# A fused retention and ELU feed-forward kernel: load costs, zero matmuls and opening order of its built-in planner

## The chip, the cores and the metric

The kernel runs on one core of one Trainium2 chip. The metric is the device time of one execution in microseconds (us), the median of several runs. Times inside an execution come from one profiled execution and count from its first instruction.

## What is computed

The reference, cut to what matters (alpha is 1):

```python
scores = (1 / sqrt(64)) * q @ k.T                 # q, k, v: batch 8, heads 8, seq 576, dim 64
Dmat   = where(rel >= 0, gamma[h] ** rel, 0.0)    # gamma[h] = 1 - 2 ** (-5 - h), rel = row - column
attn   = (scores * Dmat) @ v
x      = attn.transpose(0, 2, 1, 3).reshape(4608, 512)
h      = x @ w_in                                 # 512 x 2048
g      = where(h > 0, h, exp(min(h, 0)) - 1)
out    = g @ w_out                                # 2048 x 512, float32
```

It is a retention layer (linear attention with a decay for each head) and a feed-forward layer (FFN) behind it. Inputs and output are float32; the kernel's matmuls run in bf16.

## The kernel before

**Tiling.** The sequence of a batch is cut into two stretches of 256 positions and a tail of 64. An item is one stretch of one batch with all 8 heads; the tails of four batches form an item of their own. The four items of the first two batches are split into two units of four heads each, numbered 0 to 7; units 0 to 3 make the opening. Retention is computed in chunks of 64 positions: scores within a chunk, and a running state (the sum of k times v) that carries what lies before it. The decay is put into q and k by tables of exponentials.

**Steps of a unit n.** Loads ldq, ldk, ldv (256 KB each, queue SP, `load`, line 424, and `load_part`, line 387). Four scaled copies to bf16, cq0n, cq1n, ck0n, ck1n (line 550, POOL or DVE), and a copy of v, cvn (line 560). Two transpose steps Tn_0 and Tn_1 on TensorE, four transposes each (line 582), whose results cpn_0 and cpn_1 take from PSUM (line 588); units 5 to 7 are turned by transposing DMAs instead (trn, line 571). Then scores (scn), state (stn), masks on DVE (line 916), and the step ivn, which adds what the state and the scores with v give. For later units and items one step A does scores and state of the next and iv of the last. Two copies xc0, xc1 (line 952) put a unit's result into xt, the left operand of the FFN.

**FFN.** An FFN block has 256 rows of x (the last two 512). Step F1_b_p makes 256 columns of h for block b (8 matmuls); ACT takes the exponential (ex, line 1069), ACT or DVE a relu or the like (md), DVE combines them to g (line 1091). Step F2_b_t_f adds four matmuls of g with w_out to an output tile; a copy and a store follow. F1 of block 0 needs the xt copies of units 0 and 1; F1 of block 1 those of units 2 and 3.

**Weights.** w_in comes in five DMAs, wi0 (columns for F1_b_0), wi1 (F1_b_1), wi2 (F1_b_2 and 3), wi3 (F1_b_4 and 5), wi4 (6 and 7); w_out in four, wo0 to wo3. POOL issues all nine; they cast float32 to bf16 on the way (lines 477 to 498). Two one-element copies on POOL (line 400) wait for wo0 and wo2 and hold back the loads of units 4 and 6.

**The planner.** Nothing of the order is written out by hand. Every step is an `Op` with a cost for each engine that may do it, what it needs, and a rank. `Plan.run` (line 67) plays a list schedule with these costs at build time: on each engine that is free, the ready step of lowest rank starts (`pick`, line 100). It models the DMA queues too: a load enters 1.25 us after its issue, moves for its cost (`LD`, line 210, for a 256 KB load), and is told 0.55 us later. The result is only an order for each engine, and a choice of engine; on the chip each engine works through its list in that order and waits on semaphores for what a step needs.

`AT` (line 228) gives a due time to a named step: the plan doesn't start it sooner. `RANKS` shifts ranks. Neither waits for anything on the chip; they shape the order alone.

**Zero matmuls.** Where the plan has a gap on TensorE ahead of a step in its first 50 us, the emitting loop (lines 1210 to 1227) puts matmuls or transposes of a tile of zeros there, as fillers:

```python
gap = op.start - last if op.start < 50 and last else 0.0
...
if op.name.startswith("T"):
    for n in range(int(gap * 0.8 / 0.06)):
        pin(nc.tensor.transpose(spot[:, n % 4], zero[:, :P], ident))
elif spot is not None:
    for _ in range(int(gap * 0.8 / 0.06)):
        mm(spot[:, :P], zero[:, :P], zero[:, :P], start=True, stop=True)
```

Seven matmuls of 128x512 zeros ("warm") stand at the very start, and iv steps hold four of 64x64 as a fence. Both are apart from the fillers. All matmuls go through a helper and have line 277 in the profile; the filling transposes have line 1224.

Of the kernel before, what the change touches and what calls it, by code (L numbers as in the profile page):

```python
# [205 lines left out]
ISSUE = 0.65  # L206
JOINT = True
BD_ACT = 0.6
TWO, STEP = 2, 4
WI, WI1, LD = 1.3, 1.65, 0.84  # L210
MOST, MOSTU = 4, 3
ASKED = ("ldk0",)
BD_POOL = 0.46
# [11 lines left out]
UAPART = (5, 7)  # L225
HOLD = {"ldq4": "wo0", "ldq6": "wo2"}
VLATE = (0, 1)
AT = {"wi0": 6.0, "wi1": 10.2, "wi2": 9.4, "wi3": 11.6, "wi4": 15.0, "wo0": 17.4, "wo1": 17.4, "wo2": 19.3, "wo3": 33, "so_0_1_0_0": 74, "so_1_0_0_0": 74, "so_1_1_0_0": 74, "so_2_0_0_0": 76, "so_2_1_0_0": 81.47, "F2_3_1_0_0": 78.57, "st2": 14.97, "g_2_6": 63.17, "us7_1": 60.01, "F2_0_1_12_0": 46.64, "md_3_3": 66.87, "md_1_7": 35.82, "us5_0": 44.11, "ex_2_4": 55.85, "ex_2_2": 53.77, "xc1_u4": 43.93, "xc0_4": 82.16, "g_1_3": 27.7, "xc1_u3": 22.43, "F2_3_0_8_0": 78.02, "md_0_7": 36.11, "F1_6_6": 119.86, "tr0_5": 66.58, "md_2_2": 56.94, "ex_6_5": 119.61, "cq00": 5.78, "md_0_1": 21.97, "cp2_0": 11.19, "mask1_7": 117.16, "md_0_5": 25.96, "cp3_0": 15.79, "F2_4_0_8_0": 93.26, "cv7": 47.1, "sc1": 10.9}
RANKS = {"us1_0": -2, "F1_0_1": 4, "mask0_7": 2, "g_2_1": -2, "md_3_3": 8, "A7": -4, "cv1_5": -4, "cv1_6": 4, "mask1_u6": 8, "so_5_0_0_0": -8, "md_0_2": -8, "ex_2_7": 2, "xc0_u7": -8, "F1_2_6": -8, "A4": 2, "F2_3_0_4_0": -8}
FREE = ("f", "e", "em", "g", "ot")  # L230
SURE = 3
# [13 lines left out]
def kernel(  # L245
# [30 lines left out]
    def mm(*a, **kw):  # L276
        return pin(nc.tensor.matmul(*a, **kw))  # L277
# [59 lines left out]
    def T(cls, key, shape, dt):  # L337
        return (cls, key, shape, dt)
# [8 lines left out]
    for n, key in enumerate(ATT):  # L347
        it = Work()
# [6 lines left out]
        if not it.tail and it.b < UB:  # L355
            for w in range(2):
                u = Work()
# [63 lines left out]
    def runs(src, b, hs, T):  # L421
        return src[b, hs, TB * T : TB * (T + 1), :].rearrange("h (p e) d -> p h (e d)", e=2)

    def load(it):
        n = it.n
        shape = [P, 2 * H, D]
        if it.units:
            for u, what in [(u, what) for u in it.units for what in "qkv"] if it.n not in VLATE else \
                    [(u, what) for u in it.units for what in "qk"] + [(u, "v") for u in it.units]:
                hs = slice(4 * u.w, 4 * u.w + 4)  # L430
                if what == "q":
                    u.ld = {}
                if what == "v":
                    u.ld["v"] = load_part(
                        f"ldv{u.n}", lambda hs=hs: tiles["rv", n].rearrange("p (h e) d -> p h (e d)", e=2)[:, hs],
                        runs(v, it.b, hs, it.T), ("rv", n), u.w == 0, shape, (LD, 32))
                    continue
                i = "qk".index(what)
                u.ld[what] = load_part(
                    f"ld{what}{u.n}",  # L440
                    lambda u=u, i=i: tiles["rqk", u.n].rearrange("p (h e) d -> p h (e d)", e=2)[:, 4 * i : 4 * i + 4],
                    runs((q, k)[i], it.b, hs, it.T), ("rqk", u.n), i == 0, shape, (LD, 32))
            return
        it.ld = {}
        for name, src in (("v", v), ("k", k), ("q", q)):
# [429 lines left out]
    def after_state(it, st, tkey, off):  # L875
        if it.unit:
            return after_state_unit(it, st, tkey, off)
        for c in range(NC):
# [25 lines left out]
            def emit_b(op, skey=skey, bkey=bkey):  # L904
                pin(copy[op.eng](tiles[bkey], tiles[skey]))  # L905

            bd_op[bkey] = [add(f"bd{it.b}_{cc}", {"POOL": BD_POOL, "ACT": (0.41, BD_ACT), "DVE": (0.3, 1.5)}, [s_op], emit_b,
                               it.rank + 3, take=[T("bd", bkey, [P, HP, D], BF16)], use=[skey])]
# [236 lines left out]
    for it in items:  # L1145
        load(it)
# [33 lines left out]
    for blk in blocks:  # L1180
        base, n = (blk.at + len(blk.its)) * 16 + 1, blk.w // P
# [15 lines left out]
    for op, name in holds:  # L1197
        op.deps.append(named[name])
    for name, t in AT.items():
        if name in named:  # L1200
# [10 lines left out]
    for op in order:  # L1211
        for cls, key, shape, dt in op.take:
            pool = psum if cls == "f" else sbuf
            tiles[key] = pool.tile(shape, dt, name=cls, tag=f"{cls}{op.slot[key]}")
        fresh = [t[1] for t in op.take]
        if op.eng == "PE":
            gap = op.start - last if op.start < 50 and last else 0.0
            if gap > 0:
                spot = next((tiles[key] for key in op.use if key in tiles and (key[0] == "sc" or isinstance(key[0], tuple))), None)
                if op.take and op.take[0][0] == "f":  # L1220
                    spot = tiles[fresh[0]]
                if op.name.startswith("T"):
                    for n in range(int(gap * 0.8 / 0.06)):
                        pin(nc.tensor.transpose(spot[:, n % 4], zero[:, :P], ident))  # L1224
                elif spot is not None:
                    for _ in range(int(gap * 0.8 / 0.06)):
                        mm(spot[:, :P], zero[:, :P], zero[:, :P], start=True, stop=True)
            last = op.end
        op.emit(op)
# [33 lines left out]
```

## Time and profile before

| | us |
|---|---|
| median of 3 runs | 297.77 |
| the runs | 297.41 to 298.11 |
| the profiled execution | 297.38 |
| its span, first to last instruction | 295.6 |

The profile names engines PE (TensorE; PEld its weight loads), DVE (VectorE), ACT (ScalarE), POOL (GpSimd) and SP (SyncE, which issues most DMAs). A row of a timeline has start, duration, engine, line, operation, written tile <- read tiles, shape and count; in brackets stand the idle time before it and what ended that. Matmuls are pipelined: a row's duration holds a tail under which the next one runs, so steps are better measured by the difference of starts. A row of a view by stretches has the stretch, its length, busy time and instructions of each engine, the granted TensorE clock, the share of the 16 DMA engines and GB/s. A row of DMA issues has size and us from issue to landing. The chain of work is followed back from the last instruction, each step to what released it.

### The profile page before, as it was taken

The page shows a single profiled execution, that of the slowest core. Times are in us where ns is not written, and L with a number is a line of the kernel's source. Part 1 is how long each engine was busy: PE and PEld are TensorE (multiplying, and loading weights), DVE is VectorE, ACT ScalarE, POOL GpSimd, SP SyncE. Part 2 cuts the span into 40 slices and gives each one's busy share as a digit, 9 for nine tenths or more (in the row PEclk, how much of TensorE's full clock was granted, in tenths as well). Part 3 has the DMA queues.
Part 4 walks back from the last instruction along what each step waited for, and adds up shares of the span by engine and source line. Part 5 has one row for each costly group of instructions (what it writes and reads, how often), then busy time and mean ns, then how long its engine had stood idle before and what let it go on. Part 6 is the DMA issues. An engine that isn't in the chain of part 4 may idle for free.

```text
span 295.6 us, 9234 instructions
## 1 busy us (share of the span) xinstructions
PE 290.3 (98%) x3858; PEld 188.4 (64%) x3858; DVE 196.1 (66%) x370; ACT 162.6 (55%) x302; POOL 119.9 (41%) x190
## 2 busy tenths in 40 slices
PE   8999999999999999999999999999999999999995
PEld 5778647776586758585867576777676444444444
DVE  3987726787576948686767677787677567766500
ACT  2679506763384828374855474674664558544311
POOL 6870685753826426354733773681540000000000
PEclk9999999999999999999999999999999999999999
DMA  7999999999999977899999887976541100011221
GB/s 228 278 204 207 287 263 242 245 226 267 223 255 203 197 202 179 188 237 219 218 230 244 205 164 194 229 183 148 148 108 39 38 35 35 2 35 40 49 92 71
DMA packets 128618, 50.67 MB, mean 171 GB/s; under 512 B 92608, under 2 KB 124096, under 8 KB 128576
## 3 DMA queue, kind: packets, MB, share of 16 engines
q1 hardware_dynamic: 123296, 45.63, 65.1%
q0 software_dynamic: 4752, 4.19, 8.9%
q8 instruction: 30, 0.49, 0.7%
q10 hardware_dynamic: 528, 0.26, 0.3%
q14 instruction: 12, 0.10, 0.1%
HBM read 36.70 MB, written 9.44 MB: 156 GB/s over the span
## 4 chain that ended last, share of the span: by engine, by line
PE 95%; DMA 2%; POOL 1%; SPq 1%; issue 0%; ACT 0%; ACTq 0%
PE f L277 94%; DMA r<-in_q_dram 2%; SPq L389 1%; POOL w_in_sb L482 1%; POOL st L550 0%; PE f L582 0%; ACT ot L1130 0%; PE f L1224 0%; ACTq L1130 0%
## 5 line engine op out<-in xcount | busy, mean ns | idle before, releaser
L277 PE MATMUL f<-w_out_sb,g 128*128 128x512 bf16 (+1 forms) x592 | 138.2, 374 | 0.0
L277 PE MATMUL f<-xt,w_in_sb 128*128 128x256 bf16 (+1 forms) x1024 | 137.1, 286 | 0.0
L277 PEld LDWEIGHTS <-w_in_sb 128*128 128x128 bf16 x1024 | 99.6, 98 | 34.7
L1069 ACT ACTIVATE e<-f 128x512 f32<-128x512 f32 x144 | 85.3, 598 | 62.2 <-PE f L277 59.7
L277 PEld LDWEIGHTS <-g 128*128 128x128 bf16 x592 | 56.5, 98 | 53.6
L1083 DVE TENSOR_SCALAR em<-e 128x512 bf16<-128x512 f32 x82 | 41.7, 512 | 38.9 <-ACT e L1069 38.7
L1093 DVE SCALAR_TENSOR_TENSOR g<-f,em 128x512 bf16<-128x512 f32 x82 | 55.7, 687 | 4.9 <-DVE em L1083 0.5
L1091 DVE SCALAR_TENSOR_TENSOR g<-e,f 128x512 bf16<-128x512 f32 x62 | 41.6, 682 | 8.8 <-ACT f L1079 7.6
L607 POOL CAST kv<-r 128x512 bf16<-128x512 f32 x28 | 17.1, 629 | 56.3 <-issue 30.4
L1130 ACT COPY ot<-f 128x512 f32<-128x512 f32 (+1 forms) x37 | 21.3, 576 | 28.0 <-PE f L277 27.9
L952 ACT CAST xt<-f 128x512 bf16<-128x512 f32 (+1 forms) x37 | 21.9, 649 | 22.9 <-PE f L277 22.8
L627 POOL TENSOR_TENSOR kv<-r,gk 128x512 bf16<-128x512 f32 x28 | 29.6, 1067 | 10.3 <-DMA r<-in_k_dram 10.3
L1079 ACT ACTIVATE f<-f 128x512 f32<-128x512 f32 x56 | 33.1, 597 | 0.0
L627 POOL TENSOR_TENSOR kv<-r,gq 128x512 bf16<-128x512 f32 x28 | 30.1, 1095 | 4.6 <-DMA r<-in_q_dram 4.6
L920 DVE TENSOR_TENSOR pt<-f,mask 128x512 bf16<-128x512 f32 x28 | 18.0, 683 | 7.7 <-PE f L277 7.7
L893 DVE TENSOR_TENSOR S<-f,S 128x256 f32<-128x256 f32 x36 | 15.2, 421 | 6.7 <-PE f L277 4.2
L905 POOL CAST bd<-S 128x256 bf16<-128x256 f32 x39 | 15.3, 405 | 9.6 <-ACT S L891 3.6
L916 DVE TENSOR_TENSOR pt<-f,mask_u 128x512 bf16<-128x512 f32 x16 | 10.5, 682 | 6.1 <-PE f L277 6.0
L277 PEld LDWEIGHTS <-kv 64*64 64x64 bf16 x832 | 10.9, 104 | 0.0
L550 POOL TENSOR_TENSOR st<-r,gq 128x256 bf16<-128x256 f32 x14 | 8.6, 628 | 3.4 <-DMA r<-in_q_dram 3.4
L277 PE MATMUL f<-T 64*64 64x64 bf16 (+1 forms) x576 | 10.0, 199 | 0.0
L277 PEld LDWEIGHTS <-T 64*64 64x64 bf16 x576 | 7.6, 108 | 1.1 <-issue 0.6
(63 smaller groups left out, 127.2 us busy)
## 6 DMA issues: line engine op xcount, KB each, us to landing
r<-in_v_dram SPq DMA_DIRECT2D x32, 256.0 KB, 4.5
r<-in_k_dram SPq DMA_DIRECT2D x31, 256.0 KB, 4.4
out_dram<-ot SPq DMA_DIRECT2D x31, 256.0 KB, 2.6
r<-in_q_dram SPq DMA_DIRECT2D x12, 512.0 KB, 5.4
r<-in_q_dram SPq DMA_DIRECT2D x8, 256.0 KB, 6.0
w_out_sb<-in_moe_w_out_dram POOLq DMA_DIRECT2D x4, 512.0 KB, 10.7
w_in_sb<-in_moe_w_in_dram POOLq DMA_DIRECT2D x3, 512.0 KB, 8.8
out_dram<-ot SPq DMA_DIRECT2D x10, 128.0 KB, 2.2
```

Of the source, the lines that this page charges most:

```text
L277: return pin(nc.tensor.matmul(*a, **kw))
L607: pin(copy[op.eng](heads(tiles[nkey][:, VS[s]]), tiles["rv", n][:, s * H : (s + 1) * H]))
L627: pin(alu[op.eng].tensor_tensor(tiles[nkey][:, 2 * i + j].rearrange("p (y x d) -> p x y d", y=2, x=HP), raw.rearrange("p (x y) d -> p x y ...
L905: pin(copy[op.eng](tiles[bkey], tiles[skey]))
L920: pin(nc.vector.tensor_tensor(pt.rearrange("p h s n -> p (h s) n"), src.rearrange("p (h n) -> p h n", n=C), mask.rearrange("p e r -> p (e ...
L952: pin(copy[op.eng](dst, src))
L1069: pin(nc.scalar.activation(tiles[ekey], tiles[hkey], AF.Exp))
L1079: pin(nc.scalar.activation(ph, ph, AF.Relu))
L1083: pin(alu[op.eng].tensor_scalar_add(em, e, -1.0))
L1091: pin(nc.vector.scalar_tensor_tensor(g, e, -1.0, ph, ALU.add, ALU.min))
L1093: pin(nc.vector.scalar_tensor_tensor(g, ph, 0.0, tiles[mkey], ALU.max, ALU.min))
L1130: pin(copy[op.eng](tiles[okey][:, :width], tiles[pkey][:, :width]))
```

## The change

Constants of the planner and the filling loop; no computation is added or removed. With what follows from them, as the order of the instructions shows it:

- The cost of a 256 KB load goes from 0.84 to 0.76 us, with small corrections for three loads of units 0 and 1.
- Fillers: 0.6 of a gap in place of 0.8, and for a step that the plan starts before 6 us a filler counts as 0.107 us in place of 0.06.
- `AT` has other due times for the weight DMAs, and other steps held back. The plan made with all this has other orders on every engine. On POOL, wi0 moves behind all four scaled copies of units 0 and 1 that POOL makes, wi1 ahead of wi2, and wo3 ahead of unit 4's scaled copies and behind the tables for later items. On TensorE, F1_0_1 moves ahead of F1_0_2, and iv3 between F1_0_2 and F1_0_3; later, steps A move among F1 and F2. On ACT the exponential of F1_0_4 moves between the two xt copies of unit 3. On SP the first transposing DMA moves ahead of the loads of unit 7.

```diff
@@ -206,8 +206,9 @@
 ISSUE = 0.65
 JOINT = True
 BD_ACT = 0.6
+FILL = 0.6
 TWO, STEP = 2, 4
-WI, WI1, LD = 1.3, 1.65, 0.84
+WI, WI1, LD = 1.3, 1.65, 0.76
 MOST, MOSTU = 4, 3
@@ -225,7 +226,7 @@
 VLATE = (0, 1)
-AT = {"wi0": 6.0, "wi1": 10.2, "wi2": 9.4, "wi3": 11.6, "wi4": 15.0, "wo0": 17.4, "wo1": 17.4, "wo2": 19.3, "wo3": 33, "so_0_1_0_0": 74, "so_1_0_0_0": 74, "so_1_1_0_0": 74, "so_2_0_0_0": 76, "so_2_1_0_0": 81.47, "F2_3_1_0_0": 78.57, "st2": 14.97, "g_2_6": 63.17, "us7_1": 60.01, "F2_0_1_12_0": 46.64, "md_3_3": 66.87, "md_1_7": 35.82, "us5_0": 44.11, "ex_2_4": 55.85, "ex_2_2": 53.77, "xc1_u4": 43.93, "xc0_4": 82.16, "g_1_3": 27.7, "xc1_u3": 22.43, "F2_3_0_8_0": 78.02, "md_0_7": 36.11, "F1_6_6": 119.86, "tr0_5": 66.58, "md_2_2": 56.94, "ex_6_5": 119.61, "cq00": 5.78, "md_0_1": 21.97, "cp2_0": 11.19, "mask1_7": 117.16, "md_0_5": 25.96, "cp3_0": 15.79, "F2_4_0_8_0": 93.26, "cv7": 47.1, "sc1": 10.9}
+AT = {"wi0": 7.4, "wi1": 8.4, "wi2": 8.5, "wi3": 12.0, "wi4": 14.7, "wo0": 16.8, "wo1": 17.1, "wo2": 19.3, "wo3": 31, "so_0_1_0_0": 74, "so_1_0_0_0": 74, "so_1_1_0_0": 74, "so_2_0_0_0": 76, "so_2_1_0_0": 81.47, "F2_3_1_0_0": 78.57, "g_2_6": 63.17, "us7_1": 60.01, "md_3_3": 66.87, "md_1_7": 35.82, "us5_0": 44.11, "ex_2_4": 55.85, "ex_2_2": 53.77, "xc1_u4": 43.93, "xc0_4": 82.16, "g_1_3": 30.74, "xc1_u3": 22.43, "F2_3_0_8_0": 78.02, "md_0_7": 36.11, "tr0_5": 66.58, "md_2_2": 56.94, "md_0_1": 21.97, "mask1_7": 117.16, "md_0_5": 25.96, "F2_4_0_8_0": 93.26, "cv7": 47.1, "oc_0_1_0": 48.93, "cp1_0": 7.26, "xc1_u2": 18.95, "ex_1_5": 31.27, "us1_0": 10.35, "ub0_1": 10.62, "cq16": 39.53, "ex_0_3": 22.18, "ub2_0": 16.53}
@@ -439,7 +440,8 @@
-                    runs((q, k)[i], it.b, hs, it.T), ("rqk", u.n), i == 0, shape, (LD, 32))
+                    runs((q, k)[i], it.b, hs, it.T), ("rqk", u.n), i == 0, shape,
+                    (LD + {"q0": -0.1, "k0": 0.2, "q1": 0.05}.get(f"{what}{u.n}", 0.0), 32))
@@ -1220,10 +1222,10 @@
                 if op.name.startswith("T"):
-                    for n in range(int(gap * 0.8 / 0.06)):
+                    for n in range(int(gap * FILL / (0.107 if op.start < 6 else 0.06))):
                         pin(nc.tensor.transpose(spot[:, n % 4], zero[:, :P], ident))
                 elif spot is not None:
-                    for _ in range(int(gap * 0.8 / 0.06)):
+                    for _ in range(int(gap * FILL / (0.107 if op.start < 6 else 0.06))):
                         mm(spot[:, :P], zero[:, :P], zero[:, :P], start=True, stop=True)
```

## The prediction

> **What bounds the kernel now.** I read the page first, then the chain of work that ended last, then TensorE's timeline up to 40 us.
>
> ```profile
> span 295.6 us, 9234 instructions
> PE 290.3 (98%) x3858; PEld 188.4 (64%) x3858; DVE 196.1 (66%) x370; ACT 162.6 (55%) x302; POOL 119.9 (41%) x190
> ```
> ```profile
> 21.05 13.65 PE f L277 x128
> ...
> 58.33 171.92 PE f L277 x2700
> ...
> 230.29 62.03 PE f L277 x348
> ```
> 98% busy says little, since zeros and waiting matmuls count too. The chain (start, us, what) says more: from 21.05 to 292.3 it is TensorE alone. So the time is the moment at which TensorE becomes dense, plus a fixed amount of matmuls. The change can gain only ahead of that moment, and lose anywhere. The timeline gives the moment and the durations.
>
> ```profile
> 1.26 3.17 PE L277 MATMUL f<-zero 128*128 128x512 bf16 x7 [1.26 <-DVE zero L282]
> 4.22 2.66 PE L1224 MATMUL f<-ident,zero 128*128 128x128 bf16 x29
> 6.71 0.39 PE L582 MATMUL f<-ident,st 128*128 128x128 bf16 x4
> ...
> 15.32 0.39 PE L582 MATMUL f<-ident,st 128*128 128x128 bf16 x4
> 15.54 1.04 PE L277 MATMUL f<-xt,w_in_sb 128*128 128x256 bf16 x8
> 16.51 0.42 PE L277 MATMUL f<-T 64*64 64x128 bf16 x16
> ...
> 20.69 0.25 PE L277 MATMUL f<-T,s 64*64 64x128 bf16 x4
> 20.77 0.20 PE L277 MATMUL f<-zero 64*64 64x64 bf16 x4
> 21.05 0.25 PE L277 MATMUL f<-T,s 64*64 64x128 bf16 x4
> ...
> 21.45 10.65 PE L277 MATMUL f<-xt,w_in_sb 128*128 128x256 bf16 x96
> 31.95 2.75 PE L277 MATMUL f<-w_out_sb,g 128*128 128x512 bf16 x12
> ...
> 44.29 0.32 PE L277 MATMUL f<-vn,st 64*64 64x64 bf16 x16
> ```
> The first column is a start. From 21.45 to 31.95 stand 96 matmuls, 12 steps F1 of 0.875 each, with no hole. F1_0_4 starts at 21.45, F1_1_0 two steps later at 23.2. By start differences a transpose step T is 0.22 (15.32 to 15.54; its row has 0.39, with a tail under which the next step starts) and iv3 0.76 (20.69 to 21.45). A score step (0.42 in its row) I take as 0.35, a state step (0.32) as 0.25: estimates, the row less a shorter tail.
>
> **Part 1: fewer zeros.** By the instruction orders the fillers go from 67 (46 transposes, 21 matmuls) to 39 (23 and 16). Ahead of T0_0 they go from 29 to 4. T0_0's operands are two scaled q copies, the later one on POOL:
>
> ```profile
> 4.50 0.83 POOL L550 TENSOR_TENSOR st<-r,gq 128x256 bf16<-128x256 f32 x1 [1.65 <-DMA r<-in_q_dram]
> 5.28 0.94 POOL L482 DMA_DIRECT2D w_in_sb<-in_moe_w_in_dram  x1
> 6.24 0.63 POOL L550 TENSOR_TENSOR st<-r,gq 128x256 bf16<-128x256 f32 x1
> ...
> 9.78 1.55 POOL L482 DMA_DIRECT2D w_in_sb<-in_moe_w_in_dram  x2
> ```
> It ends at 5.33, yet T0_0 starts at 6.71: 1.3 us are zeros that overran. They go, and T0_0 starts near 5.4. The question is whether those 1.3 us reach 21.45.
>
> **Part 2: the loads don't come sooner.** Here are DMA share and GB/s (last two columns) by stretch:
>
> ```profile
> 3.00:8.00 5.00, 4.93 (x64) 3.99 (x63) 2.38 (x6) 0.94 (x3) 2.91 (x4) 1.00 1.15 343
> 8.00:10.00 2.00, 1.91 (x56) 1.40 (x50) 1.85 (x5) 1.97 (x7) 1.35 (x3) 1.00 1.29 250
> 15.00:20.00 5.00, 4.92 (x106) 3.97 (x106) 3.86 (x10) 3.23 (x7) 4.11 (x13) 1.00 1.29 204
> ```
> The DMA engines are full (share over 1) from 3 us on: 343 GB/s with q, k, v alone, 204 with w_in alone, between these when both run. F1_0_4 needs the fourth w_in transfer, wi3. Ahead of it stand the same twelve loads and three transfers as before, so its landing can't move much. Next, single issues (the last number is us to landing): v2 issued at 7.02, v3 at 7.98, wi3 at 11.89:
>
> ```profile
> r<-in_v_dram SPq DMA_DIRECT2D x1, 256.0 KB, 6.2
> r<-in_v_dram SPq DMA_DIRECT2D x1, 256.0 KB, 6.9
> w_in_sb<-in_moe_w_in_dram POOLq DMA_DIRECT2D x1, 512.0 KB, 9.4
> ```
> So v2 lands at 13.2, v3 at 14.9, wi3 at 21.3. The landing of wi3 is 0.15 ahead of F1_0_4: that is nearly all the gain there can be. For wi3 I take 21.3, with 0.5 to each side for other mixing of the two queues.
>
> New order: POOL makes four copies before it issues wi0, at 4.50 + 0.83 + 3 x 0.6 = 7.1, 1.8 later than before. A 256 KB load takes 0.262/0.343 = 0.76 us, so 1.8 us let two more loads, q3 and k3, pass ahead of w_in. Then v2 shares the engines with wi0, as q3 did. Were wi0 not in its way, v2 would land about 1.6 earlier than 13.2 (wi0's 0.262 MB at 204 GB/s is 1.3, and I add 0.3 for mixing); were it to wait for wi1 as well, 1.3 later. Bounds 11.6 and 14.5; I take 13.2, its row, since wi0 passes it again. wi1, issued at about 9.3 instead of second at 9.78 + 0.8, meets v3; v3 has bounds 13.9 (behind v2 alone) and 15.9 (all of wi1 and some of wi2 ahead); I take 15.0, nearest its row.
>
> **Part 3: TensorE's steps up to F1_0_4.** On ACT the cast of v2 comes first:
>
> ```profile
> 13.26 0.62 ACT L560 CAST vn<-r 128x512 bf16<-128x512 f32 x1 [1.86 <-DMA r<-in_v_dram]
> ...
> 21.56 0.76 ACT L952 CAST xt<-f 128x256 bf16<-128x256 f32 x2 [0.16 <-PE f L277]
> 22.54 0.60 ACT L1069 ACTIVATE e<-f 128x512 f32<-128x512 f32 x1 [0.23 <-PE f L277]
> 23.03 0.59 ACT L1079 ACTIVATE f<-f 128x512 f32<-128x512 f32 x1
> ```
> It ends at 13.88 as before. The new order has st2, sc2, T3_0 behind it (0.25 + 0.35 + 0.22, to 14.8), then F1_0_0, which waits for two casts into xt on ACT (about 0.9 after 13.9): 14.85, against 15.54. Then F1_0_0 0.88, T3_1 0.22, st3 0.25 (its cast of v3 ends at 15.65, in time), F1_0_1 0.88, sc3 0.35, iv2 0.76, fillers about 0.35: F1_0_2 at 18.6. Its w_in, wi2, is now last of the pair and lands where the pair ended before, 10.58 + 8.1:
>
> ```profile
> w_in_sb<-in_moe_w_in_dram POOLq DMA_DIRECT2D x1, 256.0 KB, 8.1
> ```
> that is 18.7. Then F1_0_2, iv3, F1_0_3 (0.88 + 0.76 + 0.88): 21.25. F1_0_4 waits for wi3 and starts at 21.35. The 0.7 won at F1_0_0 is lost to data: **gain 0.1**.
>
> **Part 4: a new wait at F1_1_0.** It needs both xt casts of unit 3. Before, ACT makes them at 21.56, ahead of F1_0_4's exponential. The new order puts that exponential between the two casts. From the rows: the exponential starts 1.09 after F1_0_4 (22.54 - 21.45), the next ACT instruction 0.49 later, the cast lasts 0.45, and about 0.07 passes to TensorE: 2.10 in all, where two F1 steps take 1.75. **Loss 0.35**, and F1_1_0 at 21.35 + 2.10 = 23.45. The four fillers put there (0.22) lie inside this wait. The bounds are 0 (ACT starts the exponential before the last matmul's end is told, which no row shows) and 0.6 (ACT is late with something else by half an exponential). Queued behind the second cast are only later exponentials, 0.5 us each, which have F1_1_0 to F1_1_7 as cover.
>
> **Part 5: the rest.** The new order moves attention steps among F1 and F2, up to 7 us; the same matmuls stay. iv5 and A6, neighbours before, are now parted by an F2 step. No row prices one turn; bounds 0 and the 0.28 from 20.77 to 21.05; I take 0.1. On SP the first transposing DMA now stands ahead of unit 7's loads, which so come up to 2.9 later (its 2.31 issue, quoted below, and one load's); A7, which needs them, is at 53, and that hides it. Other moved steps I cost at nothing: DVE and ACT, which feed them, are 66% and 55% busy, and TensorE's own dense work covers their waits. If that cover is gone somewhere, a step comes late by up to one F step, 0.9.
>
> **Sum** on the profiled execution (297.38, span 295.6): -0.1 + 0.35 + 0.1 = +0.35, 297.7. The median of the runs is 0.39 above that execution, so **298.1**.
>
> **Rivals.**
>
> *The slow pace of TensorE lasts.* Seven 512-column zeros take 2.96 us, 0.42 each; F2's twelve take 0.215 each. In the zeros alone the change is seen by weight loads (second count):
>
> ```profile
> 4.22:5.92 1.70, 1.70 (x17) 1.70 (x16) 0.00 (x0) 1.00 1.15 346
> 5.92:6.71 0.79, 0.79 (x15) 0.78 (x13) 0.00 (x0) 1.00 1.15 344
> ```
> 16 in 1.70 us, then 13 in 0.79: the pace doubles near 6.0, after 4.7 us without a hole, although the granted clock stands at 1.00 throughout. The change leaves 3.4 us without a hole, then pauses. If it stays slow until 4.7 us of F1 have run, from 14.85, then 2.3 us are lost: 300.4. Against it: at half pace the opening's steps take twice as long, fill most of 6 to 12 us, and so end the state themselves; up to 12 us there is slack. [...] Chance 0.10.
>
> *The fourth w_out transfer comes early* (a second one on the slow side). POOL issues it behind a copy that waits for w_out:
>
> ```profile
> 26.74 0.19 POOL L400 CAST r<-w_out_sb 128x1 f32<-128x1 bf16 x1 [5.62 <-DMA w_out_sb<-in_moe_w_out_dram]
> ...
> 32.42 0.61 POOL L550 TENSOR_TENSOR st<-r,gq 128x256 bf16<-128x256 f32 x1 [0.51 <-DMA r<-in_q_dram]
> 32.98 0.83 POOL L493 DMA_DIRECT2D w_out_sb<-in_moe_w_out_dram  x1
> ```
> ```profile
> 38.45 2.31 SPq L571 DMA_TRANSPOSE T<-st  x1
> ```
> ```profile
> T<-st SPq DMA_TRANSPOSE x3, 3.6
> ```
> Due times order the plan; they hold nothing on the chip. In the new order this transfer stands behind the first of these copies and the late tables (2 us), so near 29, 4 us sooner, and its data meets the loads v4 to v5, not q6 and k6. Those then come up to 2.5 us later (512 KB at 204). The transposing DMA behind them, issued at 38.45, comes between 0 and 1.7 later (2.5 less the 0.83 issue, which no longer stands ahead of POOL's copies); I take 1. It lands 3.6 after issue, 42.05; A5 starts at 44.29, in the new order an F2 step (0.87) earlier and with all else 0.35 later, so 1.7 us of delay are free. Beyond, TensorE stands still; at the full 2.5 us for 0.8: 298.9. Chance 0.12.
>
> *v3 lands late* (15.9): st3 waits 0.3 to 0.6, and all behind: 298.5. Chance 0.15.
>
> *Faster.* The runs shown reach 298.11. If the pace doubled later there, 29 zeros at 0.107 would hold T0_0 until 7.3, and the median holds 0.4 of it. The new order has no such zeros; with wi3 0.5 early: 297.1. Chance 0.13.
>
> *The change does nothing*: loads pin both dense starts, no wait at F1_1_0: 297.8. Chance 0.05.
>
> **How the numbers follow.** The forecast has 0.45. Within 0.2% (0.6 us, about what a measurement of this kernel tells from no change) lie it and the last rival: 0.50. Slower: 0.10 + 0.12 + 0.15 = 0.37. Faster: 0.13. The range 297.1 to 299.6 leaves out the slow pace and part of the fast case.
>
> **What would show it.** T0_0 near 5.4; F1_0_0 near 14.9; F1_0_4 at 21.3 to 21.5 right behind wi3; F1_1_0 near 23.45 with an xt cast as releaser; no hole later. Wrong if F1_0_4 starts under 21.0, if matmuls after 12 us are 0.11 per 128 columns, or if A5 or A6 wait for a transposing DMA.

## The result and the profile after

The changed kernel takes 298.95 us (median of 13 runs, 298.23 to 299.51), the kernel before in the same measurement 297.77 (13 runs, 297.15 to 298.62). The ratio is 1.0038, 95% interval 1.0025 to 1.0051: slower by 1.18 us, about 0.4%. The forecast was 298.1, with 297.1 to 299.6 as the range. The time lies in the range, but 0.85 above the forecast and on the side that the rivals held. (The ratios here and below leave out executions over 1.5% above the fastest of the same kernel; the only one is kernel 10's at 301.77.)

The profiled execution of after takes 299.44, span 297.7. It is 0.5 slower than its own median, so it shows 2.1 us where the medians differ by 1.18; which part of the 2.1 is this one execution's is looked at below with other kernels of the same order. First the head of the page, then TensorE's waits, but for the one for the zero tile (us in total, times, longest):

```profile
span 297.7 us, 9167 instructions
...
PE 290.1 (97%) x3830; PEld 186.7 (63%) x3830; DVE 202.6 (68%) x381; ACT 157.9 (53%) x290; POOL 120.7 (41%) x191
```
```profile
PE f L278 <- DMA w_in_sb<-in_moe_w_in_dram: 1.0, 1, 1.0
PE f L278 <- DMA T<-st: 0.4, 1, 0.4
PE f L278 <- POOL s L871: 0.4, 1, 0.4
PE f L278 <- DVE g L1095: 0.3, 1, 0.3
PE f L278 <- ACT vn L562: 0.2, 1, 0.2
PE f L584 <- POOL st L552: 0.2, 1, 0.2
```

Beside the first wait for the zero tile (1.3 in both), the kernel before had 0.2 of issue there and nothing else. The last two waits lie in the opening, at 8.33 and 11.26. TensorE's busy time is the same to 0.2 us: no work was added, it is done later. (Lines are 1 or 2 higher than before.) The end of the chain of waits (start, us, what) tells from where on nothing more is lost:

```profile
59.97 170.63 PE f L278 x2674
...
230.65 63.76 PE f L278 x356
```

From 59.97 the chain is TensorE alone, to 294.41; before it was so from 21.05. All that is new lies ahead of 60 us. The timeline tells where. The opening:

```profile
4.82 0.86 PE L584 MATMUL f<-ident,st 128*128 128x128 bf16 x4
...
14.98 1.05 PE L278 MATMUL f<-xt,w_in_sb 128*128 128x256 bf16 x8 [1.01 <-DMA w_in_sb<-in_moe_w_in_dram]
...
20.80 2.79 PE L278 MATMUL f<-xt,w_in_sb 128*128 128x256 bf16 x24
23.44 0.39 PE L278 MATMUL f<-zero 128*128 128x128 bf16 x4
23.66 0.60 PE L278 MATMUL f<-xt,w_in_sb 128*128 128x256 bf16 x4
```

T0_0 starts at 4.82 instead of 6.71, and F1_0_0 at 14.98 instead of 15.54, but F1_1_0 at 23.66, 0.45 later than before. Next, the steps A5, iv5 and the first F2 of block 2:

```profile
43.01 0.32 PE L278 MATMUL f<-vn,st 64*64 64x64 bf16 x16
43.15 0.22 PE L278 MATMUL f<-T,s 64*64 64x128 bf16 x2
43.76 0.42 PE L278 MATMUL f<-T 64*64 64x128 bf16 x16 [0.39 <-DMA T<-st]
...
47.66 0.24 PE L278 MATMUL f<-T,s 64*64 64x128 bf16 x2 [0.36 <-POOL s L871]
...
59.97 1.02 PE L278 MATMUL f<-w_out_sb,g 128*128 128x512 bf16 x4 [0.32 <-DVE g L1095]
```

A bracket counts only the idle time behind the pipeline's tail. By start differences, from the last matmul ahead of such a step to the first behind it, less the same distance where nothing waits (A5: 1.22 in before; iv5: 1.07 in 6, 10 and 12; F1, iv7 and F2: 0.97 in 3, 4 and 7), the three holes are 0.61, 0.43 and 0.38. There is a fourth loss that no bracket shows: iv5 and A6, neighbours in before, stand apart, which takes 0.22 more for the turns between them and F2. What feeds the holes stands on POOL, on SP, and among the DMA issues (one issue in each row: size, us to landing):

```profile
28.57 0.80 POOL L495 DMA_DIRECT2D w_out_sb<-in_moe_w_out_dram  x1
...
37.75 1.18 POOL L552 TENSOR_TENSOR st<-r,gq 128x256 bf16<-128x256 f32 x2 [1.56 <-DMA r<-in_q_dram]
...
45.04 1.19 POOL L552 TENSOR_TENSOR st<-r,gq 128x256 bf16<-128x256 f32 x2 [1.57 <-DMA r<-in_q_dram]
46.18 1.19 POOL L552 TENSOR_TENSOR st<-r,gk 128x256 bf16<-128x256 f32 x2
47.31 0.53 POOL L871 CAST s<-mid 128x128 bf16<-128x128 f32 x2
```
```profile
40.10 1.33 SPq L573 DMA_TRANSPOSE T<-st  x1
41.53 0.53 SPq L390 DMA_DIRECT2D r<-in_q_dram  x1
```
```profile
w_out_sb<-in_moe_w_out_dram POOLq DMA_DIRECT2D x1, 512.0 KB, 8.7
r<-in_q_dram SPq DMA_DIRECT2D x1, 256.0 KB, 9.3
T<-st SPq DMA_TRANSPOSE x1, 3.6
```

The same two q loads, of units 5 and 7, on SP in before, and the landing of the first:

```profile
28.52 0.46 SPq L389 DMA_DIRECT2D r<-in_q_dram  x1
...
34.72 0.93 SPq L389 DMA_DIRECT2D r<-in_q_dram  x1
```
```profile
r<-in_q_dram SPq DMA_DIRECT2D x1, 256.0 KB, 6.0
```

This is read as a chain. POOL issues the fourth w_out transfer at 28.57 (before: 32.98). The load ldq5, issued at 28.30, shares the DMA engines with it and takes 9.3 us instead of 6.0, so it lands at 37.6, not 34.5 (both moves of the transfer, in 3 and in 5, bear this out below). POOL's copies of unit 5 start at 37.75, so SP issues the transposing DMA tr5 at 40.10 (before: 38.45); it lands 3.6 later, at 43.7, and A5 goes on at 43.76. A5 itself reaches TensorE sooner than before, at 43.01 instead of 44.29: 44 matmuls with w_out stand ahead of it instead of 52, which is two F2 steps. On SP, ldq7 stands behind tr5 in the new order, and SP issues in order, so ldq7 waits as long as tr5 does: issued at 41.53 instead of 34.72. POOL copies unit 7 from 45.04, and behind these copies, at 47.31, stand the two small copies into s that iv5 needs. iv5 starts as they end.

The table sets all profiled kernels side by side: start of F1_0_4, of F1_1_0 and of the first matmul with w_out, the time from that to the 81st matmul with w_out (at 66 to 69 us), and the time from there to the last matmul, all in us from the trace; then the median of each in its measurement with the ratio to before there. The kernels are those of the next section.

| kernel | F1_0_4 | F1_1_0 | first w_out | to the 81st | to the end | median | ratio (interval) |
|---|---|---|---|---|---|---|---|
| before | 21.45 | 23.21 | 31.95 | 33.75 | 226.61 | 297.77 | 1 |
| after | 21.69 | 23.66 | 32.39 | 35.40 | 226.60 | 298.95 | 1.0038 (1.0025-1.0051) |
| 1 before, few zeros | 21.27 | 23.03 | 31.76 | 33.93 | 226.54 | 297.37 | 0.9997 (0.9976-1.0018) |
| 2 after, old zeros | 21.08 | 23.17 | 31.90 | 36.04 | 226.56 | 299.05 | 1.0044 (1.0028-1.0060) |
| 3 after, w_out late | 21.20 | 23.18 | 31.92 | 34.77 | 226.53 | 298.49 | 1.0032 (1.0020-1.0045) |
| 4 after, xt copy first | 21.39 | 23.37 | 32.10 | 34.87 | 226.40 | 299.02 | 1.0045 (1.0028-1.0062) |
| 5 before, w_out early | 21.45 | 23.21 | 31.94 | 35.74 | 226.60 | 299.01 | 1.0049 (1.0034-1.0064) |
| 6 after, w_out behind copies | 21.63 | 23.60 | 32.34 | 36.61 | 226.58 | 299.69 | 1.0066 (1.0044-1.0087) |
| 7 after, A5 later | 21.22 | 23.20 | 31.93 | 34.74 | 226.72 | 298.30 | 1.0019 (1.0005-1.0033) |
| 8 after, several moves | 21.45 | 23.20 | 31.93 | 35.80 | 226.62 | 298.60 | 1.0030 (1.0016-1.0043) |
| 9 as 7, s copies sooner | 21.56 | 23.54 | 32.28 | 34.54 | 226.59 | 297.97 | 1.0010 (0.9995-1.0025) |
| 10 as 9, tuned | 22.34 | 24.09 | 32.82 | 34.15 | 226.47 | 298.08 | 1.0000 (0.9980-1.0019) |
| 11 after, no zeros at F1_1_0 | 22.25 | 24.00 | 32.83 | 34.62 | 226.72 | 299.08 | 1.0041 (1.0025-1.0057) |
| 12 as 10, old zeros | 21.15 | 22.90 | 31.63 | 34.13 | 227.70 | 298.84 | 1.0030 (1.0015-1.0044) |

Three things are to be seen. The last stretch is 226.4 to 226.7 in all but one: nothing of the change acts past the 81st matmul with w_out. The opening varies from execution to execution as much as between kernels: 4 and 11 run after's own instructions up to F1_0_4, and start it at 21.39 and 22.25, where after has 21.69. The middle stretch carries the loss: 4 and 11 have after's instructions there too, and with after they give 1.65, 1.12 and 0.87 us over before, 1.2 on average, near the 1.18 that the medians lost. In all three 0.22 of it is the turns; A5's hole is 0.61, 0.58 and 0.45, iv5's 0.43, 0.29 and 0.19, and the third hole is there in after alone. 2 has the same order with more zeros and gives 2.29, with 0.96 at A6; its profiled execution was the slowest of its six. So one execution tells the size of a hole to a few tenths only.

### The profile page after: what moved, and what is told of

It is laid out like the page before. It is cut to its first block, busy times and chain, and to the rows that moved or that the text cites. A ratio compares the mean times of both kernels' runs of the same rounds, so it can differ in the third digit from the quotient of the medians.

```text
span 297.7 us, 9167 instructions
## 1 busy us (share of the span) xinstructions
PE 290.1 (97%) x3830; PEld 186.7 (63%) x3830; DVE 202.6 (68%) x381; ACT 157.9 (53%) x290; POOL 120.7 (41%) x191
## 4 chain that ended last, share of the span: by engine, by line
PE 84%; DMA 8%; POOL 3%; DVE 2%; ACT 1%; issue 1%; SPq 0%; POOLq 0%; ACTq 0%; DVEq 0%
PE f L278 84%; DMA r<-in_q_dram 5%; DMA w_in_sb<-in_moe_w_in_dram 3%; POOL st L552 2%; ACT e L1071 1%; DVE g L1093 1%; DVE em L1085 0%; DVE f L1083 0%; SPq L573 0%; DVE g L1095 0%; POOL vn L562 0%; ACT f L1081 0%; ACT ot L1132 0%; POOL s L871 0%; PE f L584 0%
## 5 line engine op out<-in xcount | busy, mean ns | idle before, releaser
L278 PE MATMUL f<-xt,w_in_sb 128*128 128x256 bf16 (+1 forms) x1024 | 140.1, 286 | 1.0 <-DMA w_in_sb<-in_moe_w_in_dram 1.0
L278 PE MATMUL f<-w_out_sb,g 128*128 128x512 bf16 (+1 forms) x592 | 140.5, 373 | 0.3 <-DVE g L1095 0.3
L1085 DVE TENSOR_SCALAR em<-e 128x512 bf16<-128x512 f32 x87 | 42.8, 492 | 41.6 <-ACT e L1071 41.5
L1095 DVE SCALAR_TENSOR_TENSOR g<-f,em 128x512 bf16<-128x512 f32 x87 | 59.4, 688 | 5.4
L1093 DVE SCALAR_TENSOR_TENSOR g<-e,f 128x512 bf16<-128x512 f32 x57 | 38.4, 683 | 8.3 <-ACT f L1081 6.9
L629 POOL TENSOR_TENSOR kv<-r,gk 128x512 bf16<-128x512 f32 x28 | 30.4, 1090 | 9.0 <-DMA r<-in_k_dram 9.0
L954 ACT CAST xt<-f 128x512 bf16<-128x512 f32 (+1 forms) x37 | 21.3, 627 | 20.5 <-PE f L278 20.4
L1081 ACT ACTIVATE f<-f 128x512 f32<-128x512 f32 x49 | 29.1, 596 | 0.0
L907 POOL CAST bd<-S 128x256 bf16<-128x256 f32 x41 | 16.0, 409 | 8.1 <-ACT S L893 4.7
```

The costliest lines, as they stand in the source:

```text
L629: pin(alu[op.eng].tensor_tensor(tiles[nkey][:, 2 * i + j].rearrange("p (y x d) -> p x y d", y=2, x=HP), raw.rearrange("p (x y) d -> p x y ...
L954: pin(copy[op.eng](dst, src))
L1081: pin(nc.scalar.activation(ph, ph, AF.Relu))
L1085: pin(alu[op.eng].tensor_scalar_add(em, e, -1.0))
L1093: pin(nc.vector.scalar_tensor_tensor(g, e, -1.0, ph, ALU.add, ALU.min))
L1095: pin(nc.vector.scalar_tensor_tensor(g, ph, 0.0, tiles[mkey], ALU.max, ALU.min))
```

## The experiments

All moves were made in the planned order, behind the planner, by one helper; lines keep their numbers.

```python
for name, engine, where, other in MOVES:
    op = named[name]
    op.eng = engine or op.eng
    order.remove(op)
    order.insert(order.index(named[other]) + (where == "behind"), op)
```

A step's gap, from which its zeros follow, moves with it; the steps in `BARE` get none. Numbers 1 to 4 shared a chip and its runs of before, so did 5 to 8 and 9 to 11; 12 ran by itself.

### Zeros and the opening: 1, 2, 4, 11

**1: before, with the new rule for zeros** (only these lines and the constant):

```diff
+FILL = 0.6
-    for n in range(int(gap * 0.8 / 0.06)):
+    for n in range(int(gap * FILL / (0.107 if op.start < 6 else 0.06))):
```

> The kernel before with the new rule for zeros alone (0.6 of a gap, 0.107 us each ahead of a step planned before 6 us); order and due times as before. Theory 'waits after the opening' (the loss is made of waits between 23 and 60 us, at F1_1_0, A5, iv5 and one F2 step, which the new order brings): the data of wi3 still decides F1_0_4 at 21.45, so F1_1_0 stays at 23.2 (within 0.2) and the median within 0.4 of 297.8. Rival 'zeros' (fewer zeros leave TensorE at its slow pace, or take the loss by gaps of their own): F1_1_0 at least 0.4 later and the median at 298.4 or above.

Measured: 297.37 against 297.56, ratio 0.9997; F1_1_0 at 23.03. **2: after, with the old rule**:

```diff
-    for n in range(int(gap * FILL / (0.107 if op.start < 6 else 0.06))):
+    for n in range(int(gap * 0.8 / 0.06)):
```

> The kernel after with the old rule for zeros (0.8 of a gap at 0.06); order as after. Theory 'waits after the opening': F1_1_0 stays near 23.66 and the median within 0.4 of 298.95. Rival 'zeros': the median falls back to 298.3 or below.

Measured: 299.05, ratio 1.0044, F1_1_0 at 23.17 (forecast near 23.66). Zeros alone neither cost nor gain anything that the medians can tell (0.2% to each side) in either kernel. In 2 the wait for a transposing DMA came a second time, at A6, which fits a chain that is late as a whole:

```profile
43.51 0.42 PE L278 MATMUL f<-T 64*64 64x128 bf16 x16 [0.43 <-DMA T<-st]
...
49.83 0.36 PE L278 MATMUL f<-T 64*64 64x128 bf16 x12 [0.89 <-DMA T<-st]
```

**4: after, xt copy ahead of the exponential.**

```diff
+MOVES = (("xc1_u3", None, "ahead", "ex_0_4"),)
```

> The kernel after with one instruction moved: on ACT the second xt copy of unit 3 ahead of the exponential of F1_0_4, as before. Theory 'waits after the opening': F1_1_0 starts two F1 steps (1.75 us) behind F1_0_4, near 23.4 instead of 23.66, and the median falls by 0.2 to 0.35, to 298.6 to 298.75. Rival (the pause is paid anyway by something behind it): F1_1_0 comes sooner, F2_0_0 or A4 stands at the same time as in the kernel after, and the median stays at 298.95.

Measured: 299.02, ratio 1.0045. F1_1_0 stays 1.98 behind F1_0_4 (after: 1.97): with the four zeros in place there had been no wait for the copy that could go. **11: after, without the four zeros ahead of F1_1_0.**

```diff
+MOVES = (); BARE = ("F1_1_0",)
```

> The kernel after without the four zeros ahead of F1_1_0, and nothing else. Theory 'the zeros are the delay there': F1_1_0 comes 1.75 to 1.80 behind F1_0_4 instead of 1.97, although the exponential still stands ahead of the second xt copy, and the median is 0.2 below that of after. The prediction's step ('the zeros lie inside a wait for the copy'): the distance stays at 1.95 to 2.1, a wait for an xt copy shows in the zeros' place, and the median stays.

Measured: F1_1_0 is 1.75 behind F1_0_4, though the copy keeps its late place. TensorE's and ACT's rows:

```profile
21.37 4.85 PE L278 MATMUL f<-xt,w_in_sb 128*128 128x256 bf16 x42
```
```profile
23.33 0.60 ACT L1071 ACTIVATE e<-f 128x512 f32<-128x512 f32 x1 [1.41 <-PE f L278]
23.82 0.44 ACT L954 CAST xt<-f 128x256 bf16<-128x256 f32 x1
```

The 42 matmuls from 21.37 are one row, but not quite without a hole. F1_1_0 begins at 24.00 among them, while the copy of unit 3 still runs until 24.26. F1 makes its 256 columns in two halves, each through the four stretches of K in order, and unit 3 fills the last two stretches: the copy is needed by the third of the eight matmuls. That one starts at 24.32, 0.21 behind the second instead of 0.11, right behind the copy. So without the zeros 0.10 of waiting for the copy appears, and the step ends only 0.12 sooner for the 0.22 of zeros taken out. 8, 10 and 12 have neither the zeros nor the late copy, and there the third matmul comes in pace. In the median it can't be told (299.08, ratio 1.0041): this opening started F1_0_4 at 22.25, a variation larger than the 0.22.

### The early transfer: 3, 5, 6

**3: after, the fourth w_out transfer back behind the first copy of unit 4.**

```diff
+MOVES = (("wo3", None, "behind", "cq04"),)
```

> The kernel after with one instruction moved: POOL issues the fourth w_out transfer behind the first scaled copy of unit 4, as before. Theory 'waits after the opening': the transfer is issued near 33, the loads of units 4 and 5 land up to 3 us sooner, the first transposing DMA is issued at 38.5 instead of 40.1, the wait of A5 for it (0.4 to 0.6) goes, and iv5's wait for a POOL copy (0.4 to 0.5), which hangs on the same chain by SP, goes as well or halves; F1_1_0 stays at 23.66; median 297.9 to 298.4. Rival 'zeros or opening': nothing in the median, 298.9. Rival 'later order' (the moves among F1 and F2 after 60 us cost the time): TensorE's last stretch stays longer, the median falls by less than 0.2.

Measured: 298.49, ratio 1.0032. The forecast of 297.9 to 298.4 is missed, and against after's 1.0038 the median shows no sure gain; the waits do what the theory says. The wait for tr5 is gone and the last hole too, that for the s copies is down from 0.43 to 0.12; ldq5 lands at 34.3 and tr5 is issued at 38.31. But a new one stands where TensorE turns unit 4:

```profile
34.38 0.29 PE L584 MATMUL f<-ident,st 128*128 128x128 bf16 x2 [0.46 <-POOL st L552]
```

POOL's 0.83 us of issuing the transfer now stands between the first and the second copy of unit 4, and in the new order F2 steps no longer cover that. By start differences 0.63 of the 1.0 left over before is this, and 0.22 the turns.

**5: before, with the transfer early.**

```diff
+MOVES = (("wo3", None, "behind", "holdldq4"),)
```

> The kernel before with one instruction moved: POOL issues the fourth w_out transfer ahead of unit 4's copies, behind the copy that holds back ldq4, as the kernel after has it. Theory 'early transfer and early A5' (the early transfer makes the first transposing DMA land near 43.7, and this costs only because the new order also has A5 an F2 step sooner and unit 7's loads behind that DMA): here A5 stands at 44.3 and covers it, so the median stays within 0.3 of 297.6, and the time between the first matmul with w_out and the 81st stays at 33.75 (within 0.3). Rival 'early transfer alone': a wait for the transposing DMA of 0.4 to 0.9 at A5 or A6, and the median at 298.2 to 298.6.

Measured: 299.01, ratio 1.0049, and 35.74 to the 81st matmul. Both miss: the median lies above the rival's 298.2 to 298.6, its waits stand at another place, and the theory's claim that the early transfer is free in the old order is wrong. TensorE, POOL, and the issue of ldq4 at 27.19:

```profile
35.61 0.28 PE L582 MATMUL f<-ident,st 128*128 128x128 bf16 x2 [0.92 <-POOL st L550]
36.18 0.28 PE L582 MATMUL f<-ident,st 128*128 128x128 bf16 x2 [0.28 <-POOL st L550]
...
37.70 0.28 PE L582 MATMUL f<-ident,st 128*128 128x128 bf16 x2 [0.26 <-POOL st L550]
```
```profile
27.43 0.80 POOL L493 DMA_DIRECT2D w_out_sb<-in_moe_w_out_dram  x1 [0.26 <-issue]
...
34.94 1.18 POOL L550 TENSOR_TENSOR st<-r,gq 128x256 bf16<-128x256 f32 x2 [2.52 <-DMA r<-in_q_dram]
```
```profile
r<-in_q_dram SPq DMA_DIRECT2D x1, 256.0 KB, 7.6
```

Here the transfer, issued 1.1 us sooner than in after, already meets ldq4, which lands at 34.8 instead of 32.3, and the transposes of unit 4 wait. A5 itself has no wait for tr5, which landed at 43.5, ahead of the 44.3 at which before reaches A5. In after the late tables hold the issue back until 28.57, ldq4 (issued 26.73) is through by 32.4, and ldq5 is the one that is hit.

**6: after, the transfer behind the third copy of unit 4.**

```diff
+MOVES = (("wo3", None, "behind", "ck04"),)
```

> The kernel after with the fourth w_out transfer moved further than in the run with it behind the first copy of unit 4: behind the third of the four, so that the first k transposes of unit 4 and the q transposes don't wait for POOL's 0.83 us of issuing. Theory: the stall of 0.46 to 0.6 at 33.7 that the earlier run brought is gone, the waits for the transposing DMA stay gone, and the median is 0.4 to 0.6 below that run's 298.5, at 297.9 to 298.1. Rival (the transfer, now issued near 34, collides with the loads of unit 6 and 7, and their steps come late): the stall at 33.7 goes, another of its size stands at iv5, A6 or A7, and the median stays at 298.4 or above.

Measured: 299.69, ratio 1.0066, the worst of all; both expectations fail. A5's row, and the issues of the transfer (34.46) and of tr5 (38.79):

```profile
45.73 0.42 PE L278 MATMUL f<-T 64*64 64x128 bf16 x16 [1.67 <-DMA T<-st]
```
```profile
w_out_sb<-in_moe_w_out_dram POOLq DMA_DIRECT2D x1, 512.0 KB, 10.4
T<-st SPq DMA_TRANSPOSE x1, 6.9
```

tr5 is issued early enough but takes 6.9 us instead of 3.6: the transfer, which lands at 44.9, is still moving when tr5 begins (see the last section). Nor is the stall at unit 4 gone: the transfer's issue now stands ahead of the fourth copy, and the second transposes wait 0.74 by start differences. So the transfer has three neighbours: too early it delays ldq4 or ldq5, a little later its issue delays POOL's copies, later still it runs into tr5. The kernel before has it at 32.98, with an order of TensorE that bears the delay of the copies.

### The order of TensorE: 7, 8, 9, 10, 12

**7: after, early transfer kept, three F2 steps moved.**

```diff
+MOVES = (("F2_1_1_8_0", None, "ahead", "A5b0"), ("F2_0_0_12_0", None, "ahead", "A5b0"),
+         ("F2_1_0_12_0", None, "ahead", "iv5b0"))
```

> The kernel after with the early transfer kept, and three F2 steps moved on TensorE: two ahead of A5 and one ahead of iv5, which is where the kernel before has them. Theory 'early transfer and early A5': A5 starts near 44.1, its wait for the transposing DMA (0.4 to 0.65) is gone or below 0.1, iv5 comes 0.9 later and its wait for a POOL copy (0.4 to 0.5) is gone as well; median 297.8 to 298.2. Rival (the late chain on SP and POOL moves all later steps, so the waits go over to A6 or iv5): the time between the first and the 81st matmul with w_out stays above 34.8, median 298.6 or above.

Measured: 298.30, ratio 1.0019, 34.74 to the 81st matmul. A5 starts at 44.3 and doesn't wait. The wait for the s copies stays, and A6, now right behind iv5, waits for an xt copy that depends on it:

```profile
47.50 0.24 PE L278 MATMUL f<-T,s 64*64 64x128 bf16 x2 [0.38 <-POOL s L871]
...
48.87 0.31 PE L278 MATMUL f<-vn,st 64*64 64x64 bf16 x14 [0.32 <-DVE xt L954]
```

So half of the theory held: A5's place costs about 0.6 with the early transfer (0.61 in after). iv5's wait doesn't come from A5; it is POOL's order, with unit 7's late copies ahead.

**8: after, those three, the transfer as in 6, holdldq6 ahead of cq04, the xt copy first, no zeros at F1_1_0.**

```diff
+MOVES = (
...
+    ("wo3", None, "behind", "ck04"), ("holdldq6", None, "ahead", "cq04"),
+    ("xc1_u3", None, "ahead", "ex_0_4")); BARE = ("F1_1_0",)
```

> The kernel after with all of it undone that the theory names: the three F2 steps moved as above, the fourth w_out transfer behind the third copy of unit 4, the copy that holds back ldq6 ahead of unit 4's copies, the second xt copy of unit 3 ahead of the exponential, and no zeros ahead of F1_1_0. The rule for zeros, the load costs and the rest of the new order stay. Theory: F1_1_0 1.75 behind F1_0_4, no wait above 0.3 between 33 and 62 us, median 297.4 to 297.8, level with the kernel before. Rival 'rest of the order': 298.3 or above with these waits gone. If the new opening were worth something, the median would be 297.2 or below.

Measured: 298.60, ratio 1.0030. F1_1_0 comes 1.75 behind F1_0_4 as expected, but the middle is 35.80: unit 4's second transposes wait 0.87 by start differences, iv5 0.38, A6 0.51, and the F2 step of the last hole 0.31. The forecast of 297.4 to 297.8 is missed. Moving the transfer behind the third copy was the wrong move, as 6 shows.

**9: as 7, with the two s copies taken from behind unit 7's copies.**

```diff
+MOVES = (
...
+    ("ub5_0", "ACT", "behind", "us5_0"), ("ck17", None, "behind", "ub5_1"),
+    ("tr7", None, "behind", "ck17"))
```

> The kernel of the run with three F2 steps moved (298.3), and in addition the two small copies that iv5 waits for out from behind unit 7's copies: the first on ACT, the second on POOL ahead of the last of the four copies of unit 7. Theory 'early transfer and tight order' (what is lost between 33 and 62 us is lost at steps that the new order puts too near to a chain over SP and POOL that the early transfer delays): iv5's wait (0.38 to 0.54 there) falls to 0.1 or less, A6 behind it keeps its wait for an xt copy (0.3 to 0.5), median 297.8 to 298.0. Rival (POOL's copies of unit 7 are the limit, so the next step of that unit, A7, waits in turn): a wait at A7 near 53, and the median stays at 298.3.

Measured: 297.97 against 298.02, ratio 1.0010. As forecast, iv5's wait is gone (it starts at 47.40), A7 has none, A6 keeps its wait for the xt copy (0.51 by start differences); 0.26 stand at the F2 step of the last hole:

```profile
48.77 0.31 PE L278 MATMUL f<-vn,st 64*64 64x64 bf16 x14 [0.29 <-DVE xt L954]
```

**10: as 9, one more F2 step ahead of A6, the xt copy first, no zeros at F1_1_0.**

```diff
+MOVES = (
...
+    ("F2_1_1_12_0", None, "ahead", "A6b0"),
+    ("xc1_u3", None, "ahead", "ex_0_4")); BARE = ("F1_1_0",)
```

> All of the run before in this list, and in addition one more F2 step ahead of A6, no zeros ahead of F1_1_0, and the second xt copy of unit 3 ahead of the exponential; the fourth w_out transfer stays early. Theory: no wait of TensorE above 0.15 between 21 and 60 us; F1_1_0 1.75 behind F1_0_4, and the time from the first to the 81st matmul with w_out at 33.7 to 33.9, as before the change; median 297.2 to 297.5, as fast as the kernel before or 0.1% faster. Rival 'rest of the order': these waits gone and the median at 298 or above.

Measured: 298.08, ratio 1.0000 (0.9980 to 1.0019). All waits from F1_0_4 to 60 us above 0.2 are gone, and it takes 34.15 to the 81st matmul. So within the 0.2% of the interval the loss of the change is undone by moving eight steps and leaving out four zeros, with its load costs, its opening and its early transfer in place. The forecasts of 297.2 to 297.5 and of 33.7 to 33.9 are missed: 0.40 over before remain in the middle, 0.22 of it the turns of iv5 and A6, which stand apart here too, and 0.17 a wait at A7. The rival's 298 or above fits by its number, but before read 298.02 there. But the opening of this execution was the slowest of all. TensorE by stretches (the granted clock is the number behind the busy times):

```profile
7.00:7.80 0.80, 0.61 (x18) 1.00 1.15 345
7.80:8.40 0.60, 0.60 (x20) 0.63 1.15 346
8.40:14.20 5.80, 5.80 (x99) 0.50 1.25 272
...
14.60:20.00 5.40, 5.32 (x144) 0.98 1.25 206
```

The clock was 0.50 with TensorE busy throughout, from 7.96 (the 0.63 of the second row) to 14.8 (the 0.98 of the last), and F1_0_0 started at 15.75. What came ahead of it:

```profile
4.22 0.55 PE L1226 MATMUL f<-ident,zero 128*128 128x128 bf16 x4
5.38 0.28 PE L584 MATMUL f<-ident,st 128*128 128x128 bf16 x2 [0.61 <-DVE st L552]
5.85 0.28 PE L584 MATMUL f<-ident,st 128*128 128x128 bf16 x2 [0.19 <-POOL st L552]
```

The first loads were 0.5 us late in this execution, four zeros don't reach that far, and the transposes come in pieces with pauses of 0.6 and 0.2. The mean clock over the span tells such executions: 0.986 to 0.994, for 6.8 us at half pace in 297 make 0.989, and half of that 0.994. Of the eleven executions of kernel 10 in the ratio four are such, at 298.49 to 299.43; the other seven have 297.23 to 298.49, median 297.58. With 9 and 11 on the same chip it is 7 of 31; of 25 executions of the kernel before there, none. After's own 13 had none, and of the 48 of kernels 3, 4, 6, 7 and 8 on another chip there was one. So the forecast's rival "the slow pace of TensorE lasts" has a relative that is real and mostly rare: the pace does not last, it comes back.

**12: as 10, with the old rule for zeros** (ten zero transposes ahead of T0_0).

> The kernel with all waits moved away (298.08, equal to before on the same chip, but 297.2 to 297.7 in its executions with the clock at 0.998 or above and 298.5 or more in four with 0.986 to 0.994), now with the old rule for zeros, still with none ahead of F1_1_0. Ten zero transposes stand ahead of T0_0 in place of four. Theory 'few zeros let some executions open at half pace' (where the first loads land late, TensorE pauses before T0_0 and between its transposes, and the pace doubles only near 14 us): no execution below 0.995, median 297.4 to 297.7, ratio to before 0.998 to 1.0. Rival 'the late clock is the chip's own': executions at 0.99 as often as there (5 in 12), median near 298, on a chip where the run before it had them.

Measured: no execution below 0.998, which goes with the theory, but on another chip, where no kernel with few zeros ran beside it; that the zeros prevent the low clock is therefore possible, not shown. The time missed both expectations: 298.84, ratio 1.0030. In its profile the opening is the best of all and the middle the best of the new orders (first w_out at 31.63, 34.13 to the 81st), and 1.1 us are lost at one spot late in the dense part:

```profile
192.15 0.93 PE L278 MATMUL f<-xt,w_in_sb 128*128 128x256 bf16 x7
194.01 0.27 PE L278 MATMUL f<-xt,w_in_sb 128*128 128x256 bf16 x1 [0.94 <-issue]
```

In the middle of a step, between its seventh and eighth matmul, TensorE waits for nothing that the profile shows. No other kernel here has such a hole. It has 18 matmuls and 18 weight loads more than kernel 10, but 2 has 20 matmuls more than after, and no such hole; the cause is open. No version was found that is surely faster than the kernel before.

## Why the prediction was right or wrong

**Part 1, zeros: right.** T0_0 started even earlier (4.82 instead of 5.4), and the 1.9 us won there reach nothing; 1 and 2 show from both sides that the rule for zeros is worth nothing that the medians can tell. TensorE's pace doubled near 7.0 instead of 6.0 (0.107 us from one transpose to the next until then), and the slack of the opening took that too.

**Part 2, loads: right where it counts.** wi3 landed at 21.4 (forecast 21.3). v2 landed at 11.4, just below the bound of 11.6: wi0's data began to move only near 10.7, when v2 was nearly through. wi0 in turn came at 14.9, and the wait of 1.01 at F1_0_0 was not forecast. In this execution it had a cost: F1_0_4 started 0.28 behind the landing of wi3, where 3, 4, 7, 8 and 9, whose wi0 came by 13.7, have it 0.04 to 0.15 behind.

**Part 3, F1_0_4: right within its spread.** Forecast 21.35; the eleven profiles with the new opening have 21.08 to 22.34, middle value 21.45, the three with the old one 21.27 to 21.45. The gain is 0, not 0.1. The forecast had no term for the spread, which is the half-pace opening at its upper end in one of them.

**Part 4, F1_1_0: half right in its mechanism, near the right size.** The forecast put 0.35 on a wait for the second xt copy, with the four zeros inside it. The copy ended when it was forecast (2.01 after F1_0_4; forecast 1.09 + 0.49 + 0.45), but the step needs it at its third matmul, 0.22 later than the forecast had it. So the wait alone is 0.10 (11), and the zeros, 0.22, are longer than the wait and set the delay; 4 shows that moving the copy alone gains nothing.

**Part 5 failed.** "Other moved steps I cost at nothing" and "A7, which needs them, is at 53, and that hides it" looked for those who need unit 7's loads, and not for those who stand behind them on POOL. Nor did ldq7 come up to 2.9 later, but 6.8: it waits on SP until tr5 can be issued, and by the forecast's own row that is 38.45 at best. The step that was late is iv5: the s copies behind unit 7's copies cost 0.43. The turns of iv5 and A6 were forecast, at 0.1 with 0.28 as the bound; they took 0.22. The same part weighed the third hole, an F2 step late by up to 0.9, and gave it no cost; it took 0.38 in this execution, 0.31 and 0.26 in 8 and 9, and is absent in 3, 4, 7 and 11, which have the same F2 order there.

**The fourth w_out transfer** was a rival with 0.12; it is what happened, by the mechanism told. tr5 was issued 1.65 later (forecast 0 to 1.7), landed at 43.7, and A5 lost 0.61 (priced 0.8 at most). The step that failed is the slack. The forecast read A5 as one F2 step (0.87) earlier in the new order and so held 1.7 us of delay to be free; it is two steps earlier, as 7 shows by putting two back, and by its own working about 0.85 was free. The forecast's own sentence, that due times hold nothing on the chip and that the transfer stands behind only one copy and 2 us of tables, gave 29 us as the issue time (measured 28.57); with two steps in the slack even the 1 us that it took for tr5 would have cost 0.15, and its bound of 1.7 about 0.85.

**The sum.** Forecast +0.35. In the profiled execution: +0.24 at F1_0_4, +0.21 at F1_1_0, +0.61 at A5, +0.43 at iv5, +0.38 at F2, +0.22 for the turns, together +2.09, the difference of the spans to 0.01. By the medians of the kernels with the same order the lasting part is about 1.2: A5, iv5 and the turns. That the time lies in the range is in part luck: the range was wide enough for losses that the forecast itself put elsewhere or at nothing.

## What to carry to other kernels

The DMA that was issued 4.4 us sooner here cost a load queued beside it its pace: ldq5 took 9.3 us in place of 6.0. When a transfer moves, look for the load beside it whose consumer has no slack, and for everybody who stands behind that consumer on the same engine's list (here the s copies, behind unit 7's copies on POOL, 0.43 at iv5), not only for those who need the data. A due time in this plan binds only if an instruction ahead of it waits (wo3, due at 31, was issued at 28.57): ask what on the engine really holds it. Filling work in an opening whose end is set by data cost nothing here that the medians can tell (1: 0.9997; 2: 1.0044 beside after's 1.0038); whether it guards the clock against loads that come late is not shown.

## What the runs showed of the hardware

**The long packets of a transposing DMA ended together.** In the packet records of before, 11 packets of 256 B of tr5 took over 0.4 us: they start between 40.98 and 41.72 us and all end between 42.14 and 42.20, the longest after 1.2. In after none took over 0.23. In kernel 6, 21 such packets start between 40.6 and 43.7 us and all end between 44.64 and 44.68, the longest after 4.1 us; in kernel 3 twenty such end between 41.99 and 42.02. The last packet of the w_out transfer ended at 40.4 in before and 36.9 in after, ahead of tr5's first (40.5 and 41.4); in 6 the transfer landed at 44.9. What holds the packets is not shown. Kernel 6 by stretches of 2 us moves 57 GB/s from 42 to 44, where before has 287.

**In kernel 10 the clock fell in the opening without any long pause.** It went from 1.00 to 0.50 near 8 us with no pause of TensorE over 0.61 ahead of it (0.61, 0.19, 0.18 and 0.18), and came back only near 14.8, after 6.8 us at 0.50 without a hole; 2.6 of them (11.6 to 14.2) were transposes. Kernel 9 opened with pauses of 0.18, 0.19 and 0.19 and had 1.00 in every stretch to 20 us; kernel 6, with 0.32, 0.18, 0.19 and 0.19, has a mean clock of 0.998 over its span. So what tips it, and what brings it back, is open.

**The same instructions landed their loads at different times.** With one and the same opening, in the profiles of after and of the kernels made from it, wi0 landed between 13.4 and 15.0 us after issues at 7.4 to 8.0, and F1_0_0 started between 13.9 and 15.8.
